# Dilated sliding-window attention and a swish MLP: list-scheduled order on shared PSUM banks, with direct and crossbar loads and half-row scores

## The chip, the cores and the metric

The kernel runs on one core of a Trainium2 chip. The metric is the time of one execution on the device in microseconds; the kernel before takes 364.86 us, the median of three runs (363.77 to 367.04). All times below that are not that median come from one profiled execution of 364.4 us. The engines are called PE (TensorE, matrix products), ACT (ScalarE), DVE (VectorE), POOL (GpSimd) and SP (the engine that issues most DMAs).

## The reference

Two steps. First attention for 8 batches, 8 heads, 576 positions, 64 features per head, in which each head sees 32 keys only:

```python
rel = pos[:, None] - pos[None, :]
mask_plain = (rel >= 0) & (rel < 32)                     # heads 0 to 3
mask_dil = (rel >= 0) & (rel < 128) & (rel % 4 == 0)     # heads 4 to 7
scores = np.where(mask, q @ k.T / 8.0, -1e9)
attn = softmax(scores)                                   # over the keys
attn_out = attn @ v                                      # (8, 8, 576, 64)
```

Then its result, laid out as x with 4608 tokens of 512 features, goes through an MLP with 2048 hidden units and a gate with one beta for each unit:

```python
h = x @ w_in                                             # 512 -> 2048
g = h * (1 / (1 + exp(-beta * h)))
out = g @ w_out                                          # 2048 -> 512
```

Inputs and output are fp32. Both kernels multiply in bf16 and use 0.5 (1 + tanh(beta h / 2)) for the sigmoid.

## The kernel before

The MLP works on nine tiles of 512 tokens ("stages", t = 0 to 8). For each tile there are 16 blocks of hidden units; a block is four 512-column matmuls, a tanh on ACT, and a gate on DVE:

```python
def slot_h(t, fb):
    hps = bank() if t == 0 and fb % 3 else psum_h.tile([P, NTOK], FP32, name="h_ps")[:]
    for kt in range(NKT):                                # 4
        nc.tensor.matmul(hps, lhsT=w_in_bf[:, kt, fb * P:(fb + 1) * P],
                         rhs=xT[:, kt, t * NTOK:(t + 1) * NTOK], ...)
    nc.scalar.activation(out=tnh[:], in_=hps, func=ACT.Tanh, scale=beta_half[:, fb:fb + 1])
    nc.vector.scalar_tensor_tensor(out=g[:], in0=tnh[:], scalar=1.0, in1=hps, op0=ALU.add, op1=ALU.mult)
```

Then four output blocks of 128 tokens, 16 matmuls of 512 columns each, with a copy out of PSUM and a store (`slot_o`, in four parts). Part of the output blocks is put off into the next stage: `at_once = [4, 2] + [1] * (NTT - 3) + [4]` says how many blocks a stage does itself.

Attention of batch 0 runs ahead of all this. Attention of batch t + 1 is cut into steps that are laid between the MLP's slots of stage t, in a fixed list of names. Index x = 0, 1 stands for the two pairs of plain heads, x = 2, 3 for the two pairs of dilated heads, for which positions are split by their remainder mod 4, so that the dilated window becomes a plain one.

```python
STEPS = ("K0 Q0 K1 Q1 S00 S01 S02 S10 V00 S11 V01 S12 X00 V10 S20 X01 V11 S21 X10 S22 V20 X11 S23 "
         "V21 S30 V22 X20 S31 V23 S32 V30 X21 S33 V31 V32 X30 V33 X31").split()
```

- K, Q (plain heads): fp32 loads into a staging buffer, a cast (POOL), eight PE transposes of 72 columns, a copy out of PSUM. Q is written twice, into a tile whose other half is zero (`qz`), so that one matmul with 128 rows gives the scores of both heads of a pair side by side.
- K, Q (dilated heads): a casting DMA into a DRAM scratch (`cast_dil`), then a DMA that transposes on its way into SBUF (`load_dil`), then a copy of Q into the zero-padded `qzd` (`spread_dil`).
- S: scores, exp, mask.
- V: values, with a column of ones that gives the softmax's sum; reciprocal; normalisation.
- X: PE transposes back into the feature-by-token layout of xT, and a copy.

```python
def step_s(b, x, j):
    ...
    for a in range(2):          # n = 96 (plain) or 72 (dilated), both heads side by side: 2 n columns
        nc.tensor.matmul(sc[:, a, 0:2 * n], lhsT=lhsT, rhs=rhs, start=True, stop=True)
    nc.scalar.activation(out=w, in_=sc[:, :, 0:2 * n], func=ACT.Exp, scale=SCALE)
    eng = nc.gpsimd if b > 1 else nc.vector
    eng.tensor_tensor(out=w, in0=w, in1=mask, op=ALU.mult)

def step_v(b, x, j):
    n, m = (QT, 3) if x < 2 else (HT, 2)
    for a in range(m):
        for h2 in range(2):
            ...
            nc.tensor.matmul(pv[:, a, h2, :], lhsT=pt[x][:, c:c + P], rhs=rhs, start=True, stop=True)
    nc.vector.reciprocal(out=rcp[0:n, 0:m], in_=pv[0:n, :, :, D])
    nc.vector.tensor_tensor(out=xs[...], in0=pv[0:n, :, :, 0:D], in1=rcp[...], op=ALU.mult)
```

PSUM has eight banks, given away by use: two for h, one for output blocks, five for attention.

```python
psum_h = psum("psum_h", 2)
psum_o = psum("psum_o", 1)
psum_at = psum("psum_at", 5)
```

The start, in the order of the program: plain K and Q of batch 0 (fp32, SP), casts of dilated K and Q of batches 0 and 1 into DRAM, their transposing loads, V, masks, and only then `load_w_in`; attention 0; `load_w_out`.

Of the kernel before, what the change touches and what calls it, by code (L numbers as in the profile page):

```python
# [13 lines left out]

STEPS = (
    "K0 Q0 K1 Q1 S00 S01 S02 S10 V00 S11 V01 S12 X00 V10 S20 X01 V11 S21 X10 S22 V20 X11 S23 "
    "V21 S30 V22 X20 S31 V23 S32 V30 X21 S33 V31 V32 X30 V33 X31"
).split()  # L20


STEPS_FIRST = (
    "K0 Q0 K1 S00 Q1 S01 S02 S10 S11 S12 S20 S21 S22 S23 S30 V00 S31 V01 S32 X00 "
    "V10 S33 X01 V11 V20 X10 V21 X11 V22 X20 V23 V30 X21 V31 V32 X30 V33 X31"
).split()
# [3 lines left out]
def kernel(  # L30
# [10 lines left out]
    nc = tc.nc  # L41
# [5 lines left out]
    SCALE = 1.0 / 8.0  # L47
    WIN = 32
    C = 4
    CT = S // C  # L50
    HT = CT // 2
    R = 8
    RT = S // R
# [6 lines left out]
    WG = 512  # L60
    FROM = 4
    DV = 96
    GATES = (1,)

    pool = lambda name, bufs: ctx.enter_context(tc.tile_pool(name=name, bufs=bufs))
    psum = lambda name, bufs: ctx.enter_context(
        tc.tile_pool(name=name, bufs=bufs, space=bass.MemoryType.PSUM))
    ctx.enter_context(tc.manual_schedule())

    const_pool = pool("const", 1)  # L70
    stage_pool = pool("stage", 1)
    qkb_pool = pool("qkb", 1)
    dil_pool = pool("dil", 2)
    dram_pool = ctx.enter_context(tc.tile_pool(name="dram", bufs=1, space=bass.MemoryType.DRAM))
    xs_pool = pool("xs", 2)
    rcp_pool = pool("rcp", 4)
    g_pool = pool("g", 2 * NFB)
    tnh_pool = pool("tnh", 3)
    osb_pool = pool("osb", 2)
    psum_h = psum("psum_h", 2)  # L80
    psum_o = psum("psum_o", 1)
    psum_at = psum("psum_at", 5)

    def bank(dt=FP32):
        b = psum_at.tile([P, 512], FP32, name="at")
        return b[:] if dt == FP32 else b[:].bitcast(BF16)

    const = lambda shape, dt, name: const_pool.tile(shape, dt, name=name)
    w_in_bf = const([P, NKT, DFF], BF16, "w_in_bf")
# [5 lines left out]
    mask_p = {n: const([P, 2, 2, C, QT // C], BF16, f"mask_{n}") for n in ("FP", "PP")}  # L95
    mask_d = [const([P, 2, 2, HT], BF16, f"mask_d{hf}") for hf in range(2)]
    kT = [const([P, WIN + S], BF16, f"kT{x}") for x in range(2)]

    qz = [const([P, 2, S], BF16, f"qz{x}") for x in range(2)]
    qzd = [const([P, 2, 2, 4, CT], BF16, f"qzd{i}") for i in range(2)]  # L100
    pt_w = [NI * 2 * QT, NI * 2 * QT, 8 * 2 * HT, 8 * 2 * HT]
    pt = [const([P, pt_w[x] + 64], BF16, f"pt{x}") for x in range(4)]
    vp = [const([P, NI, 4, DV], BF16, f"vp{i}") for i in range(2)]
    vd = [const([P, 2, 4, C, DV], BF16, f"vd{i}") for i in range(2)]
    vp_st = const([P, NI, 4, D], FP32, "vp_st")
    vd_st = const([P, 2, 4, C, D], FP32, "vd_st")
    xT = const([P, NKT, B * S], BF16, "xT")
    warm = const([P, 1], FP32, "warm")
    gate_t = const([1, 16], BF16, "gate_t")


    def zeros():
        nc.vector.memset(warm[:], 0.0)
        nc.scalar.activation(out=warm[:], in_=warm[:], func=ACT.Exp)
        for x in range(4):
            nc.vector.memset(pt[x][:, pt_w[x]:], 0.0)
            if x < 2:
                nc.vector.memset(kT[x][:, 0:WIN], 0.0)
                nc.vector.memset(qz[x][64:128, 0], 0.0)
                nc.vector.memset(qz[x][0:64, 1], 0.0)  # L120
        for i in range(2):
            nc.vector.memset(qzd[i][64:128, 0], 0.0)
            nc.vector.memset(qzd[i][0:64, 1], 0.0)
            nc.vector.memset(vp[i][:, :, :, D:D + 1], 1.0)
            nc.vector.memset(vd[i][:, :, :, :, D:D + 1], 1.0)
            nc.vector.memset(vd[i][96:128, 0, :, :, 0:D], 0.0)
        nc.vector.memset(vp[0][0:WIN, 0, 0, 0:D], 0.0)
        nc.vector.memset(vd_st[96:128, 0], 0.0)

    def build_masks():  # L130

        pp = mask_p["PP"]
        flat = pp[:].rearrange("p a b T u -> p (a b) T u")
        nc.gpsimd.memset(flat, 1.0)
        nc.gpsimd.affine_select(
            out=flat, in_=flat, pattern=[[0, 4], [-1, C], [-C, QT // C]], base=-1,
            channel_multiplier=1, compare_op=ALU.is_ge, fill=0.0)
        nc.gpsimd.affine_select(
            out=flat, in_=flat, pattern=[[0, 4], [1, C], [C, QT // C]], base=WIN,
            channel_multiplier=-1, compare_op=ALU.is_ge, fill=0.0)  # L140
        nc.vector.tensor_copy(out=mask_p["FP"][:], in_=pp[:])
        nc.vector.memset(mask_p["FP"][0:WIN, 0], 0.0)

        for hf, lo in ((0, 0), (1, HT - 16)):
            flat = mask_d[hf][:].rearrange("p a b n -> p (a b) n")
            nc.gpsimd.memset(flat, 1.0)
            nc.gpsimd.affine_select(
                out=flat, in_=flat, pattern=[[0, 4], [1, HT]], base=lo,
                channel_multiplier=-1, compare_op=ALU.is_ge, fill=0.0)
            nc.gpsimd.affine_select(  # L150
                out=flat, in_=flat, pattern=[[0, 4], [-1, HT]], base=WIN - 1 - lo,
                channel_multiplier=1, compare_op=ALU.is_ge, fill=0.0)

    def build_beta():
        tpb = bank()
        nc.tensor.transpose(tpb[:, 0:NFB], beta_row[:, :], ident_f[:, :])
        nc.vector.tensor_single_scalar(
            out=beta_half[:], in_=tpb[:, 0:NFB], scalar=0.5, op=ALU.mult)

    def load_w_in(g):  # L160
        nc.gpsimd.dma_start(
            out=w_in_bf[:, :, g * WG:(g + 1) * WG],
            in_=moe_w_in[:, g * WG:(g + 1) * WG].rearrange("(c p) d -> p c d", p=P))

    def load_w_out(g):
        nc.gpsimd.dma_start(
            out=w_out_bf[:, g * 4:(g + 1) * 4, :],
            in_=moe_w_out[g * 4 * P:(g + 1) * 4 * P, :].rearrange("(c p) d -> p c d", p=P))


    stage, qkb = {}, {}

    def load_qk(b, kind):
        src = {"q": q, "k": k}[kind][b, 0:4].rearrange("h (t T) d -> t h (T d)", T=R)
        dst = stage[b, kind] = stage_pool.tile([RT, 4, R * D], FP32, name=f"{kind}_st")

        for lo, hi in ((0, 64), (64, RT)) if b < 2 else ((0, RT),):
            nc.sync.dma_start(out=dst[lo:hi], in_=src[lo:hi])


    scratch, dil = {}, {}

    def cast_dil(b, kind):
        dst = scratch[b, kind] = dram_pool.tile([CT, 4 * C * D], BF16, name=f"{kind}d{b}")
        nc.gpsimd.dma_start(
            out=dst[:], in_={"q": q, "k": k}[kind][b, 4:8].rearrange(
                "h s d -> (h s d)").rearrange("(a e) -> a e", e=4 * C * D))


    def load_dil(b, kind):  # L190
        dst = dil[b, kind] = dil_pool.tile([P, 2, 4, CT], BF16, name=f"{kind}dT")
        nc.sync.dma_start_transpose(  # L192
            out=dst[:].rearrange("p r h t -> p r (h t)"),
            in_=scratch[b, kind][:].rearrange("a e -> (a e)").rearrange("(a e) -> a e", e=C * D))

    def spread_dil(b, eng):
        for hf in range(2):
            rows = slice(64 * hf, 64 * hf + 64)
            eng.tensor_copy(out=qzd[b % 2][rows, hf], in_=dil[b, "q"][rows])  # L199


    def cast_qk(b, kind, hp, eng):
        if hp == 0:
            qkb[b, kind] = qkb_pool.tile([RT, 2, R, 2, D], BF16, name=f"{kind}b0")
        for h2 in range(2):
            (eng.copy if eng is nc.scalar else eng.tensor_copy)(  # L206
                out=qkb[b, kind][:, hp, :, h2, :],
                in_=stage[b, kind][:, 2 * hp + h2].rearrange("p (T d) -> p T d", T=R))


    def plain_v(b, h4):
        return bass.AP(tensor=v.tensor, offset=v[b, h4].offset - WIN * D,
                       ap=[[D, P], [QT * D, NI], [1, D]])


    def load_vp(b):
        for h4 in range(4):
            if b > 1:
                nc.sync.dma_start(out=vp_st[:, :, h4, :], in_=plain_v(b, h4))
            elif b or h4:  # L220
                nc.gpsimd.dma_start(out=vp[b][:, :, h4, 0:D], in_=plain_v(b, h4))
            else:
                src = v[b, h4].rearrange("(i p) d -> p i d", p=QT)
                nc.gpsimd.dma_start(out=vp[b][WIN:P, :, h4, 0:D], in_=src)
                nc.gpsimd.dma_start(
                    out=vp[b][0:WIN, 1:NI, h4, 0:D], in_=src[QT - WIN:QT, 0:NI - 1])
# [16 lines left out]

    def gate(t, fb):
        nc.sync.dma_start(out=gate_t[:], in_=g_t[t, fb][0:1, 0:16])


    def transposes(b, x, kind):
        src = qkb[b, kind]
# [281 lines left out]
```

The softmax here doesn't subtract the row's maximum and nothing guards it: scores larger than these inputs give would overflow.

## Time and profile before

The page gives busy time of each engine, the span in 40 slices, the chain of work that ended last, and groups of instructions. The lines that the prediction reads are shown there. Beside them these rows are used:

| what | count | mean of one | from |
|---|---|---|---|
| MLP matmul, 512 columns | 1152 in the program | 215.7 ns apart in a stream | chain, four in 0.86 us |
| tanh, 128x512 | 144 | 687 ns | groups |
| gate, 128x512 | 144 | 686 ns | groups |
| exp, 128x384 and 128x288 | 48 and 64 | 487 and 411 ns | groups by shape |
| mask on POOL, 128x384 and 128x288 | 36 and 48 | 936 to 998 and 727 ns | groups by shape |
| normalisation, 96x384 and 72x256 | 32 and 64 | 554 and 421 ns, plus 186 and 174 for the reciprocal | groups by shape |
| copy to xT, 128x288 | 64 | 397 ns | groups by shape |
| output block out of PSUM | 36 | 597 ns | groups |
| DMA over the span | 66,751 packets, 45.8 MB | 45,968 under 512 bytes | page |

A matmul's own mean (384 ns) is its latency; the distance between the starts of two is what a stream costs. A busy share is an average over stages that differ much, so the prediction reads the stages one by one.

### The profile page before, as it was taken

The page shows a single profiled execution, that of the slowest core. Times are in us where ns is not written, and L with a number is a line of the kernel's source. Part 1 is how long each engine was busy: PE and PEld are TensorE (multiplying, and loading weights), DVE is VectorE, ACT ScalarE, POOL GpSimd, SP SyncE. Part 2 cuts the span into 40 slices and gives each one's busy share as a digit, 9 for nine tenths or more (in the row PEclk, how much of TensorE's full clock was granted, in tenths as well). Part 3 has the DMA queues.
Part 4 walks back from the last instruction along what each step waited for, and adds up shares of the span by engine and source line. Part 5 has one row for each costly group of instructions (what it writes and reads, how often), then busy time and mean ns, then how long its engine had stood idle before and what let it go on. Part 6 is the DMA issues. An engine that isn't in the chain of part 4 may idle for free.

```text
span 364.4 us, 6201 instructions
## 1 busy us (share of the span) xinstructions
PE 315.1 (86%) x2305; PEld 167.3 (46%) x2305; DVE 205.2 (56%) x440; ACT 197.1 (54%) x380; POOL 149.8 (41%) x204
## 2 busy tenths in 40 slices
PE   0266999885977999989999999899989999999995
PEld 0254455442443555545554545454545444444442
DVE  6477488556641966485648565756576635334400
ACT  1373486354651776567656755575657545435511
POOL 8444740364285438453936493549243200000000
PEclk9999999999996999999999999999999999999998
DMA  7999999898937950983099419831101110111032
GB/s 180 167 242 210 221 205 149 216 219 216 221 76 188 232 81 23 215 222 78 29 220 250 93 33 233 221 82 30 31 29 31 29 31 29 42 47 29 29 75 72
DMA packets 66751, 45.77 MB, mean 126 GB/s; under 512 B 45968, under 2 KB 57248, under 8 KB 66464
## 3 DMA queue, kind: packets, MB, share of 16 engines
q1 hardware_dynamic: 55728, 35.67, 40.8%
q0 software_dynamic: 10992, 9.70, 17.0%
q8 instruction: 18, 0.29, 0.4%
q14 instruction: 13, 0.11, 0.1%
HBM read 40.89 MB, written 14.16 MB: 151 GB/s over the span
## 4 chain that ended last, share of the span: by engine, by line
PE 67%; DMA 10%; DVE 7%; POOL 6%; ACT 4%; issue 3%; SPq 2%; POOLq 0%; ACTq 0%
PE o_ps L376 28%; PE h_ps L345 26%; DMA w_in_bf<-in_moe_w_in_dram 3%; POOL pt L292 3%; DVE qzd L199 3%; PE at L345 3%; DMA qdT<-qd 3%; PE at L306 3%; SPq L192 2%; PE at L288 2%; DMA vd_st<-in_v_dram 2%; DVE g L353 2%; PE h_ps L376 2%; PE at L322 2%; POOL qb L206 2%
## 5 line engine op out<-in xcount | busy, mean ns | idle before, releaser
L353 DVE SCALAR_TENSOR_TENSOR g<-tnh,h_ps 128x512 bf16<-128x512 bf16 x134 | 91.3, 686 | 105.6 <-ACT tnh L350 105.2
L345 PE MATMUL h_ps<-xT,w_in_bf 128*128 128x512 bf16 x536 | 138.4, 384 | 12.0 <-DVE g L353 9.7
L376 PE MATMUL o_ps<-w_out_bf,g 128*128 128x512 bf16 x544 | 139.2, 384 | 2.9 <-ACT osb L381 2.9
L350 ACT ACTIVATE tnh<-h_ps,beta_half 128x512 bf16<-128x512 f32 x134 | 92.1, 687 | 69.6 <-PE h_ps L345 67.2
L345 PEld LDWEIGHTS <-w_in_bf 128*128 128x128 bf16 x576 | 52.7, 99 | 60.4 <-issue 15.7
L376 PEld LDWEIGHTS <-g 128*128 128x128 bf16 x576 | 52.6, 99 | 53.0 <-issue 6.1
L290 ACT ACTIVATE pt<-at 128x288 bf16<-128x288 f32 (+1 forms) x112 | 47.2, 443 | 11.9 <-PE at L288 11.9
L292 POOL TENSOR_TENSOR pt<-pt,mask_d 128x288 bf16<-128x288 bf16 x48 | 34.9, 727 | 41.0 <-ACT pt L290 35.1
L313 DVE TENSOR_TENSOR xs<-at,rcp 72x256 bf16<-72x256 f32 (+1 forms) x96 | 44.6, 465 | 3.3
L306 PEld LDWEIGHTS <-pt 128*128 128x128 bf16 x448 | 26.3, 103 | 20.4 <-POOL pt L292 8.0
L381 ACT ACTIVATE osb<-o_ps 128x512 f32<-128x512 f32 x34 | 20.3, 597 | 27.2 <-PE o_ps L376 27.2
L292 POOL TENSOR_TENSOR pt<-pt,mask_PP 128x384 bf16<-128x384 bf16 x24 | 22.3, 936 | 21.5 <-ACT pt L290 21.4
L332 ACT COPY xT<-at 128x288 bf16<-128x288 bf16 x32 | 12.7, 397 | 26.0 <-PE at L322 26.0
L322 PE MATMUL at<-ident_b,xs 72*128 72x72 bf16 (+1 forms) x224 | 21.6, 209 | 5.7 <-DVE xs L313 5.7
L292 POOL TENSOR_TENSOR pt<-pt,mask_FP 128x384 bf16<-128x384 bf16 x12 | 12.0, 998 | 35.2 <-ACT pt L290 35.2
L309 DVE RECIPROCAL rcp<-at 72x4 f32<-72x4 f32 (+1 forms) x96 | 17.1, 178 | 15.6 <-PE at L306 14.8
L306 PE MATMUL at<-vd,pt 128*128 128x65 bf16 x256 | 19.9, 201 | 6.8 <-POOL pt L292 6.8
L206 POOL CAST kb<-k_st 72x512 bf16<-72x512 f32 x28 | 16.3, 610 | 17.9 <-PE at L306 17.9
L322 PEld LDWEIGHTS <-xs 72*128 72x128 bf16 (+1 forms) x224 | 15.5, 101 | 17.2 <-DVE xs L313 7.7
L239 POOL CAST vd<-vd_st 128x2048 bf16<-128x2048 f32 x8 | 15.3, 1914 | 10.5 <-DMA vd_st<-in_v_dram 10.5
L288 PE MATMUL at<-qzd,kdT 128*128 128x144 bf16 x128 | 18.6, 238 | 0.7 <-DVE qzd L199 0.7
L206 POOL CAST qb<-q_st 72x512 bf16<-72x512 f32 x28 | 16.3, 610 | 4.8 <-DMA q_st<-in_q_dram 4.8
(64 smaller groups left out, 229.0 us busy)
## 6 DMA issues: line engine op xcount, KB each, us to landing
vp_st<-in_v_dram SPq DMA_DIRECT2D x24, 192.0 KB, 6.7
vd_st<-in_v_dram SPq DMA_DIRECT2D x8, 512.0 KB
k_st<-in_k_dram SPq DMA_DIRECT2D x6, 576.0 KB
q_st<-in_q_dram SPq DMA_DIRECT2D x6, 576.0 KB
vd_st<-in_v_dram SPq DMA_DIRECT2D x8, 384.0 KB
kd<-in_k_dram POOLq DMA_DIRECT2D x8, 288.0 KB, 7.7
qd<-in_q_dram POOLq DMA_DIRECT2D x8, 288.0 KB, 8.7
w_in_bf<-in_moe_w_in_dram POOLq DMA_DIRECT2D x4, 512.0 KB, 16.1
```

The costliest lines, as they stand in the source:

```text
L206: (eng.copy if eng is nc.scalar else eng.tensor_copy)(out=qkb[b, kind][:, hp, :, h2, :], in_=stage[b, kind][:, 2 * hp + h2].rearrange("p ( ...
L288: nc.tensor.matmul(sc[:, a, 0:2 * n], lhsT=lhsT, rhs=rhs, start=True, stop=True)
L290: nc.scalar.activation(out=w, in_=sc[:, :, 0:2 * n], func=ACT.Exp, scale=SCALE)
L292: eng.tensor_tensor(out=w, in0=w, in1=mask, op=ALU.mult)
L306: nc.tensor.matmul(pv[:, a, h2, :], lhsT=pt[x][:, c:c + P], rhs=rhs, start=True, stop=True)
L313: nc.vector.tensor_tensor(out=xs_t[b, x, jx][:, a0:a0 + m], in0=pv[0:n, :, :, 0:D], in1=rcp[0:n, 0:m].unsqueeze(3).to_broadcast([n, m, 2, ...
L322: nc.tensor.transpose(xp[:, a * n:(a + 1) * n], xs[:, a].rearrange("p h d -> p (h d)"), ident_b[0:n, 0:n])
L345: nc.tensor.matmul(hps, lhsT=w_in_bf[:, kt, fb * P:(fb + 1) * P], rhs=xT[:, kt, t * NTOK:(t + 1) * NTOK], start=(kt == 0), stop=(kt == NKT ...
L350: nc.scalar.activation(out=tnh[:], in_=hps, func=ACT.Tanh, scale=beta_half[:, fb:fb + 1])
L353: nc.vector.scalar_tensor_tensor(out=g[:], in0=tnh[:], scalar=1.0, in1=hps, op0=ALU.add, op1=ALU.mult)
L376: nc.tensor.matmul(ops[:], lhsT=g_t[t, fb][:, tb * P:(tb + 1) * P], rhs=w_out_bf[:, fb, :], start=(fb == 0), stop=(fb == NFB - 1))
L381: nc.scalar.mul(out=osb[:], in_=ops[:], mul=0.5)
```

## The change

Nearly all of the kernel is written anew around the same computation. The program no longer lists its instructions: it describes operations with their dependencies, durations and the PSUM bank that each needs, and a planner (`Plan`) places them, when the program is built, by priority and earliest start.

```diff
+class Plan:
+    CAPS = {"h": 3, "p": 4, "o": 2, "z": 4, "a": 8, "s": 5, "w": 6}
+    SWITCH = 95
+    NUDGE = {32: -900, 54: 400, 98: -900, 188: -60, ... 1057: -60}
+    LAT = {"PE": 210, "ACT": 45, "DVE": 45, "POOL": 60, "SP": 0}
+    NEAR = {"PE": 40, "ACT": 60, "DVE": 60, "POOL": 60, "SP": 0}
...
-    psum_h = psum("psum_h", 2)
-    psum_o = psum("psum_o", 1)
-    psum_at = psum("psum_at", 5)
+    BANKS = [psum_pool.tile([P, 512], FP32, name=f"bank{i}") for i in range(8)]
+    plan = Plan(range(8))
...
+    act = lambda n: ("ACT", 175 + .834 * n)
+    dve = lambda n: ("DVE", 160 + 1.042 * n)
+    mm = lambda n: n / 2.4 + 2.5
```

All eight banks are shared; CAPS bounds how many each kind of use may hold. Copies and masks may go to either of two engines, whichever ends first by the plan. While PE waits in the first 80 us of the plan, it runs filler matmuls on zeros:

```diff
+    def filler(b):
+        nc.tensor.matmul(BANKS[b][:, 0:256], lhsT=zero[:, 0:P], rhs=zero[:], start=True, stop=True)
+    plan.run(filler, 80000.0)
```

Loads. Batches 0 to 2 (`DIRECT = 3`) load q, k and v with casting DMAs issued by POOL right into bf16 tiles (the first dilated keys by SP in fp32, and a cast), and transpose K and Q on PE: per batch 24 transposes of 96 columns (dilated) and 72 of 64 columns on 64 rows (plain). Batches 3 to 7 cast q and k of all heads into DRAM scratch, and four crossbar DMAs transpose them into SBUF. A small POOL copy that reads an earlier result (`t_pace`) holds back each batch's loads.

```diff
+    def cast(b, z, h0, deps, vt):
+        dst = scratch[b, z, h0] = dram_pool.tile([S * 4 * D], BF16, name=f"s{b}_{z}_{h0}")
...
+        if h0:     # dilated heads: long runs
+            args = [x.rearrange("(a c e) -> c a e", c=16, e=1024) for x in ...]
+        else:      # plain heads: runs of 64
+            args = (dst[:].rearrange("(s h d) -> s h d", h=4, d=D), src.rearrange("h s d -> s h d"))
+    def crossbar(b, z, h0, deps, vt):
...
+        src = scratch[b, z, h0][:].rearrange("(a e) -> a e", e=C * D)
+        return plan.op([("SP", 1300)], lambda e: nc.sync.dma_start_transpose(out=dst, in_=src), ...)
```

Scores. Q is no longer padded with zeros. Each matmul contracts over the 64 rows of one head, and the two heads of a pair stand in the upper and the lower 64 rows, each with its own PSUM bank:

```diff
+    for c in range(2):
+        rows = slice(64 * c, 64 * c + 64)
+        nc.tensor.matmul(bank(gs[2 * n + c])[:, i * P:(i + 1) * P], lhsT=dk[kv][rows, r, h4, 0:P],
+                         rhs=dq[kv][rows, r, h4, 0:P], start=b >= ADDED, stop=b >= ADDED or i == 3)
```

Dilated heads now take 128 of their 144 positions in one tile of queries and keys; the last 16 queries of each remainder, with the 48 keys that they can see, go into an extra tile for two remainders at once (steps T, U, Y: four matmuls of 68 columns, eight of 65, two transposes). Per batch there are 16 half-row matmuls of 128 columns and 24 of 96. From batch 2 on (`PAIRED`) the score steps of two pairs of heads are done together, from batch 3 on (`AT_ONCE`) all the plain scores at once. The masks of batch 0 are added in PSUM by identity matmuls with -65536 outside the window (`ADDED = 1`; only the tail tile keeps a multiplied mask); later batches multiply after the exp, on POOL or DVE.

The way back. Batches 0 and 1 transpose on PE as before. From batch 2 on (`BY_DMA = 2`) normalised rows are stored into DRAM and come back into xT through a crossbar DMA, in two halves of 288 positions:

```diff
+    o = plan.op([("SP", 1300)], lambda e: nc.sync.dma_start_transpose(out=cols, in_=rows[:]), out + dil, ...)
```

Start and end. The planner puts w_in (three loads, the first of 512 columns) behind batch 0's loads, then batch 1's loads, then w_out (two loads). In stage 0 the first four blocks of hidden units (`APART = 4`) start with the dilated half of x. The last output block is computed and stored in three pieces of columns. Tokens keep their natural order in x, so every output block is one store.

## The prediction

> **What bounds the kernel now.** I read the page in the order busy shares, slices, chain, then cut the span at the places where one token tile of the MLP ends (a stage) and asked for busy time and PE waits in each piece.
>
> The page's busy line and its slices:
>
> ```profile
> PE 315.1 (86%) x2305; PEld 167.3 (46%) x2305; DVE 205.2 (56%) x440; ACT 197.1 (54%) x380; POOL 149.8 (41%) x204
> PE   0266999885977999989999999899989999999995
> PEclk9999999999996999999999999999999999999998
> ```
>
> TensorE is the bound from slice 13 on; before that (9.1 us a slice) it stands at 0, 2, 6, 6 and dips again at slices 9, 11 and 12. No other engine is over 56%. The chain says which waits are on the path:
>
> ```profile
> PE 67%; DMA 10%; DVE 7%; POOL 6%; ACT 4%; issue 3%; SPq 2%; POOLq 0%; ACTq 0%
> ```
>
> And in the chain's pieces in order of time, the two long DMA pieces: the first weights, behind the first attention's loads, and a transposing load of the third batch's queries.
>
> ```profile
> 24.99 11.71 DMA w_in_bf<-in_moe_w_in_dram
> ...
> 76.01 9.78 DMA qdT<-qd
> ```
>
> The stage windows (us, then busy us and count of PE, PEld, DVE, ACT, POOL, then granted clock, DMA share, GB/s):
>
> ```profile
> 0.00:36.70 36.70, 13.38 (x145) 10.57 (x145) 23.31 (x72) 14.47 (x32) 20.02 (x38) 1.00 1.12 200
> 36.70:76.00 39.30, 37.30 (x276) 19.51 (x277) 24.90 (x60) 22.00 (x44) 15.44 (x22) 1.00 1.10 200
> 76.00:117.10 41.10, 32.42 (x239) 16.87 (x237) 22.23 (x46) 20.31 (x42) 23.35 (x30) 0.88 0.86 186
> 220.90:256.90 36.00, 33.87 (x274) 18.44 (x272) 22.79 (x46) 22.42 (x44) 19.25 (x25) 1.00 0.51 130
> 292.90:360.20 67.30, 65.89 (x304) 29.55 (x302) 22.00 (x32) 28.55 (x43) 0.00 (x0) 1.00 0.15 44
> ```
>
> The unit of account: four 512-column matmuls follow each other in 0.86 us (the chain), 215.7 ns each. The MLP has 9 x 128 of them, 248.5 us, in either kernel. A full stage is 128 x 215.7 ns = 27.6 us. So the time before splits into 248.5 of MLP and 115.9 of everything else: **head** 36.7 (first MLP matmul); **stage 0** 39.3 - 27.6 = 11.7; **stage 1** holds only 96 of its matmuls (one 32-block is left for stage 2), 41.1 - 20.7 = 20.4; **stage 2** (112 matmuls, ends 149.7) 32.6 - 24.2 = 8.4; **stages 3 to 6** 36.0 + 35.2 + 36.0 + 36.0 - 4 x 27.6 = 32.8; **stages 7 and 8** 67.3 - 304 x 0.2157 = 1.7; **tail** 4.2. Sum 115.9.
>
> In a later stage the overhead is 8.4 us. Its small matmuls can be counted (head pair x = 0..3): K and Q 32 transposes of 72 columns, scores 12 x 192 and 16 x 144, values 56 x 65, back 12 x 96 and 16 x 72. By the formula n/2.4 + 2.5 ns that is 1.04 + 0.99 + 1.00 + 1.66 + 1.03 = 5.7 us. The remaining 2.7 us are waits and ends of batches: the PE waits in that stage name 1.4 us for DVE's gate and 0.7 for POOL's mask.
>
> **What the Trainium skill says.** "TensorE: Matmul & The Clock Gate", section "Wait — 56ns, not 53.3ns?": a warm stream starts a matmul every n/2.4 + 2.5 ns. The trace agrees also for small ones: eight 72-column transposes take 0.26 us (32.5 ns each), six 65-column value matmuls 0.185. The same page, Part 1: an idle array is given half its clock. The trace has two such spells, 3.4 and 6.8 us long, both in stage 1 (its 0.88 above). "TensorEngine Tiling (Array Packing)", section "Key Properties": different tiles run in parallel, and changing the tiling mode drains the array; no tiled matmul is in this trace. "DMA: Bandwidth & Descriptors", Specifications: under 512 B a transfer falls below line rate. The trace's packet records agree: 2048 B packets took 119 ns (17 B/ns), 256 B ones 23 ns (11 B/ns), casting ones that write 128 B 33 ns.
>
> **The change, part by part.**
>
> *Head.* Before, TensorE starts the MLP at 36.7: attention 0 ran from 10.4 (first cast) to 34.9 (last copy to xT), and w_in was issued only at 25.0. After, loads are issued at once, cast on the way into SBUF, and w_in follows batch 0. Costs from the packet records on 16 engines: a 576 KB fp32 load cast in big packets 23.6/16 = 1.48 us; both weights 25.2 us, so 12.6 for w_in and 3.2 for its first quarter; the 2304 small packets of the plain V 2304 x 33 / 16 = 4.8 us. So K and Q 5.9, dilated V about 1.8, plain V 4.8, first w_in 3.2: 15.7, and some 3 us of issue and landing: **19**. ACT and DVE work of attention 0, at their rows' rates (576-column evacuation 0.75, 512-column exp 0.6, 288-column 0.41, normalisation 0.6 to 0.74, xT copy 0.4), sums to about 22 us; over two engines, starting near 7 us, it ends at 18 if nothing waits. The chain K, S, exp, V, norm, X, copy is long, so I add 5: the MLP starts at **23**, a gain of 13.7.
>
> *Attention on TensorE.* Half-row scores use 64 rows, two heads side by side: if pairs overlap, a batch costs 8 x 55.8 + 12 x 42.5 = 0.96 us plus 4 x 31 = 0.12 for the tail of 16 keys, instead of 1.99. Values: 48 x 29.6 = 1.42 instead of 1.66. From batch 3 on (crossbar) K and Q transposes go; from batch 2 on the transposes back go. With the diff's own allowance of 95 ns a mode change, a crossbar batch is 0.96 + 0.12 + 1.42 + 4 x 0.095 = **2.9 us** against 5.7. Batches 1 and 2 still transpose: dilated 24 x 42.5 = 1.02, plain 72 x 29.2 = 2.10. Batch 1: 1.02 + 2.10 + 1.08 + 1.42 + back 1.02 + 12 changes 1.1 = **7.7**; batch 2 without back and with six changes: **6.1**. So the first two stages gain nothing in PE work; what they can gain is waits.
>
> *Waits.* Stages 0 and 1 lost 11.7 - 5.7 = 6 and 20.4 - 5.7 = 14.7 us beyond attention (DMA of batch 2, clock, POOL masks). Eight pooled banks, a planned order and filler matmuls should take most; I leave 3.5 each. Later stages: 2.7 becomes 1.3 (choice: half). Last two stages 1.5, tail 3.2 (the last block is evacuated in parts).
>
> Sum: 23 + (27.6 + 7.7 + 3.5) + (27.6 + 6.1 + 3.5) + 5 x (27.6 + 2.9 + 1.3) + 55.3 + 1.5 + 3.2 = **318 us**.
>
> *Other engines in a 31.8 us stage.* ACT: 16 tanh x 0.69 + exps 5.8 + four outputs 2.4 = 19; DVE: 16 gates x 0.69 + norms 5.8 + some masks = 18 to 22; POOL: masks up to 11 plus issuing 8. None reaches 31.8.
>
> **Rivals.** (1) *DMA becomes the bound.* A crossbar batch costs, by packet records: dilated casts 2 x 1.48, plain casts to DRAM in 64-element runs 2 x 4.8, four crossbars of 1152 packets 4 x 1.65, V 1.8 + 1.6 + 4.8, back writes and crossbars about 5.8, output 3.8: 37 us against a 31.8 us stage. For: that sum, and two queues at a share of 1.1 in the first 76 us. Against: those packets were timed while queues shared the engines (a share over 1 means overlap), so alone they are shorter; and the stage from 220.9 shows 0.51 x 36.0 = 18 us of packets, so DMA has half of each stage free to begin with. If true, about 5 us in each of five stages: 343. (2) *Half-rows don't overlap*, or each change drains more: 1 to 2 us a stage, 326. (3) *The MLP start is held by attention 0* as now, because its chain and not the loads set it: 30 instead of 23, so 325. (4) *The loads were hidden anyway and the planned order mistimes an engine*: a fixed order waits where the plan's durations are wrong; every engine waits for the latest. At 2 us a stage, 335. (5) Better than planned: waits nearly gone, start at 20: 305.
>
> **Range and chances.** To be slower, the change would have to give back 47 us; even rivals 1 and 2 together leave 351. Range 304 to 340, skewed up for the DMA. Faster by over 2% 0.95, within 2% 0.02, slower 0.03.
>
> **What would show it.** First MLP matmul near 23; crossbar stages 31 to 32.5 us apart; PE waits naming DMA in the crossbar stages would speak for rival 1; starts of paired half-row matmuls closer than 10 ns for the overlap; no half-clock spell before the end. The prediction is wrong if stages 2 to 6 come out at 35 us or the start past 30.

## The result, and the profile after

The changed kernel takes **304.44 us** (median of four, 304.37 to 304.52) against 364.31 before in the same comparison: ratio 0.8347, 95% interval 0.8299 to 0.8394. The prediction was 318, range 304 to 340; the time lies just above the range's lower edge.

The page of the kernel after, its busy line, three slice rows and the chain by engine:

```profile
PE 292.8 (97%) x2271; PEld 150.7 (50%) x2307; DVE 187.8 (62%) x424; ACT 170.3 (56%) x306; POOL 88.5 (29%) x126
...
PE   7989999999999999999999999999999999999995
...
PEclk9999999999999999999999999999999999999999
DMA  7999999799769999995699989996160100010122
...
PE 89%; DVE 6%; issue 2%; DMA 1%; ACT 0%; SPq 0%; DVEq 0%
```

TensorE is busy for 90% or more of every slice (7.6 us each) from the fourth to the last but one, and the row of its granted clock shows no drop. DMA's share of the chain went from 10% to 1%, although its engines are full in most slices up to 225 us. The windows after (same columns as before: us; PE, PEld, DVE, ACT, POOL busy and counts; clock; DMA share; GB/s). I cut them where DMA's work changes, because the planner mixes the stages:

```profile
0.00:19.70 19.70, 16.33 (x231) 11.69 (x232) 13.01 (x44) 10.37 (x22) 17.50 (x37) 1.00 1.18 180
19.70:55.00 35.30, 34.51 (x389) 20.02 (x393) 26.44 (x66) 25.09 (x53) 18.30 (x27) 1.00 1.39 201
...
111.30:146.50 35.20, 34.72 (x265) 17.31 (x269) 24.67 (x62) 19.57 (x36) 9.59 (x12) 1.00 1.19 165
...
225.00:299.70 74.70, 74.33 (x371) 35.54 (x376) 27.95 (x42) 34.12 (x53) 0.00 (x0) 1.00 0.12 43
299.70:302.80 3.10, 0.03 (x1) 0.00 (x0) 0.29 (x1) 0.17 (x1) 0.00 (x0) 1.00 0.29 91
```

And all waits of TensorE from the first MLP matmul to the end, the five groups that the trace names (us in total, times, longest):

```profile
PE bank L903 <- issue: 0.8, 5, 0.2
PE bank L728 <- DVE g L882: 0.5, 1, 0.5
PE bank L664 <- ACT kT L239: 0.2, 1, 0.2
PE bank L868 <- issue: 0.2, 1, 0.2
PE bank L664 <- DVE g L882: 0.2, 1, 0.2
```

1.9 us in 280. In the prediction's account the profiled 302.8 us are: head 19.8 (first MLP matmul, the line below); 279.9 from there to 299.7, of which 248.5 is the MLP and **31.4** everything else; tail 3.1.

```profile
19.77 1.09 PE L868 MATMUL bank<-xT,w_in_bf 128*128 128x512 bf16 x3
```

Of the 61.6 us between the two profiled spans, the head gave 36.7 - 19.8 = 16.9, the tail 1.1, and the overhead inside the MLP 75.0 - 31.4 = 43.6 (before: 11.7 + 20.4 + 8.4 + 32.8 + 1.7). How much of these 43.6 is less work on TensorE can be estimated in two ways. By the count of small matmuls, seven batches at 5.7 us are 39.9 before, against 27.1 after (28.3, less two terms named below), so 13 us are work and 31 are waits and lost clock. By the windows, TensorE was idle for 21.7 us from 36.7 to 360.2 before and lost 5 at half clock (0.88 over 41.1 us), and was idle for 3.6 from 19.7 to 299.7 after, so 23 are waits and clock and 20 are work. Waits and clock are the larger part either way.

### The profile page after: what moved, and what is told of

Its sections match the earlier page's. It is cut to its first block, busy times and chain, and to the rows that moved or that the text cites. A ratio compares the mean times of both kernels' runs of the same rounds, so it can differ in the third digit from the quotient of the medians.

```text
span 302.8 us, 5972 instructions
## 1 busy us (share of the span) xinstructions
PE 292.8 (97%) x2271; PEld 150.7 (50%) x2307; DVE 187.8 (62%) x424; ACT 170.3 (56%) x306; POOL 88.5 (29%) x126
## 4 chain that ended last, share of the span: by engine, by line
PE 89%; DVE 6%; issue 2%; DMA 1%; ACT 0%; SPq 0%; DVEq 0%
PE bank L903 40%; PE bank L868 39%; DVE g L882 2%; PE bank L785 2%; DMA beta_row<-in_moe_beta_dram 1%; PE bank L664 1%; PE bank L769 1%; PE bank L692 1%; PE bank L466 1%; PE bank L473 1%; DVE xdm L620 1%; DVE ptt L604 1%; PE bank L654 1%; PE bank L754 1%; PE bank L728 1%
## 5 line engine op out<-in xcount | busy, mean ns | idle before, releaser
L877 ACT ACTIVATE tnh<-bank,beta_half 128x512 bf16<-128x512 f32 x144 | 97.6, 690 | 71.4 <-PE bank L868 68.6
L903 PE MATMUL bank<-w_out_bf,g 128*128 128x512 bf16 (+2 forms) x588 | 136.2, 367 | 1.6 <-issue 0.8
L868 PE MATMUL bank<-xT,w_in_bf 128*128 128x512 bf16 (+1 forms) x568 | 136.1, 376 | 1.0 <-issue 0.2
L882 DVE SCALAR_TENSOR_TENSOR g<-tnh,bank 128x512 bf16<-128x512 bf16 x144 | 97.3, 686 | 62.2 <-ACT tnh L877 61.4
L918 ACT ACTIVATE osb<-bank 128x512 f32<-128x512 f32 (+1 forms) x34 | 20.0, 588 | 31.2 <-PE bank L903 30.4
L600 ACT ACTIVATE pt<-bank 128x384 bf16<-128x384 f32 (+1 forms) x54 | 20.4, 466 | 6.4 <-PE bank L692 4.3
L600 ACT ACTIVATE ptd<-bank 128x512 bf16<-128x512 f32 x32 | 16.6, 602 | 6.6 <-PE bank L664 6.6
L620 DVE TENSOR_TENSOR xsp<-bank,rcp 96x384 bf16<-96x384 f32 x32 | 17.7, 554 | 1.1
L390 POOL DMA_DIRECT2D vp<-in_v_dram x9 | 15.3, 1696 | 0.4 <-DVE dkt L239 0.4
L785 PEld LDWEIGHTS <-pt 128*128 128x128 bf16 x192 | 8.8, 97 | 4.7
## 6 DMA issues: line engine op xcount, KB each, us to landing
s<-in_q_dram POOLq DMA_DIRECT2D x10, 288.0 KB, 9.4
s<-in_k_dram POOLq DMA_DIRECT2D x10, 288.0 KB, 6.5
vp<-in_v_dram POOLq DMA_DIRECT2D x7, 288.0 KB, 17.1
st<-in_q_dram POOLq DMA_DIRECT2D x6, 288.0 KB, 9.8
st<-in_k_dram POOLq DMA_DIRECT2D x5, 288.0 KB, 11.2
```

Of the source, the lines that this page charges most:

```text
L390: {"POOL": nc.gpsimd, "SP": nc.sync}[queue].dma_start(out=out, in_=in_)
L600: nc.scalar.activation(out=w(), in_=sc(), func=ACT.Exp, scale=SCALE)
L620: nc.vector.tensor_tensor(out=dst, in0=p[..., 0:D], in1=r.unsqueeze(len(p.shape) - 1).to_broadcast(list(p.shape[:-1]) + [D]), op=ALU.mult)
L785: nc.tensor.matmul(pv[:, a, h2, :], lhsT=lhs, rhs=vp[kv][:, (2 * x + h2) * NI + 3 * j + a, 0:D + 1], start=True, stop=True)
L868: nc.tensor.matmul(bank(g)[:, a:z], lhsT=w_in_bf[:, kt, fb * P:(fb + 1) * P], rhs=xT[:, kt, xo + a:xo + z], start=(i == 0 and kt == kts[0] ...
L877: nc.scalar.activation(out=th[:, 0:n], in_=bank(g)[:, 0:n], func=ACT.Tanh, scale=beta_half[:, fb:fb + 1])
```

## The experiments

What is in question: did the gain come from less work on TensorE (half rows, crossbar), from waits taken away (banks, order, fillers), or from the loads; and how near was rival 1, the DMA? "Between" below is the time from the first MLP matmul to the last one's end, 279.9 us in the kernel after; it leaves the head out, which varies (last section).

### Half rows

```diff
-rows = slice(64 * c, 64 * c + 64)      # one_half: for the upper head too
+rows = slice(0, 64)
-rows = slice(64 * c, 64 * c + 64)      # full_rows
+rows = slice(0, 128)
```

> The changed kernel in the same planned order, but both heads of a pair take their scores from the lower 64 rows (so the scores of every second head are those of its neighbour: the output is not the reference's). The mode and the number of instructions stay, only the two halves can't run side by side. Theory, the pairs overlap and TensorE is the bound: 8 x 55.8 + 12 x 42.5 = 0.96 us more in each of seven batches, +6.7, so 311. Rival, such work fits into waits that exist anyway: below 306.

> As the run with one half, but every score matmul contracts over all 128 rows (so it adds up the scores of two heads: the output is not the reference's): no overlap and no change of mode. If a change of mode costs the 95 ns that the plan allows, 38 changes in the batches after the head give back 3.6 us: 307.5. If a change costs nothing, 311 as with one half.

One half: 310.05 us (ratio to before 0.8475, 0.8429 to 0.8521), full rows 306.93 (0.8386, 0.8333 to 0.8439). The same step in the kernel after and then in the run with one half, start and length:

```profile
80.22 0.62 PE L664 MATMUL bank<-dq,dk 64*128 64x128 bf16 x16
```

```profile
81.24 1.06 PE L664 MATMUL bank<-dq,dk 64*128 64x128 bf16 x16
```

The same 16 matmuls take 0.44 us less when neighbours use different halves; the prediction's 8 x 55.8 = 0.45. In the trace of the kernel after, the two matmuls of a pair start 3 or 4 ns apart. Between grew by 6.6 us to 286.5, as the 6.7 expected; the timed 5.6 is smaller by the head, which was 0.8 us shorter in the profile. So the pairs overlap fully, and TensorE is the bound: work put on it shows in the time. Full rows take 2.2 us less than one half between, and one wait of 1.1 us for a load stands against them. The 38 changes of mode that were expected are not what the traces hold. Counted there from the first MLP matmul on (one matmul on 64 rows next to one on more), there are 44 changes with one half and 14 with full rows, which are left by transposes on 64 rows. So 30 changes cost 2.2 to 3.3 us, 73 to 110 ns each. The Trainium skill, "TensorEngine Tiling (Array Packing)", Key Properties, says that a change drains the array; this is its price here. Half rows as a whole, overlap minus changes, are worth 306.93 - 304.44 = 2.5 us by the times, but 4.4 by between (284.3 against 279.9), or 3.3 without that wait; the head of the profile with full rows is 1.7 us shorter.

```diff
-    PAIRED = 2
-    AT_ONCE = 3
+    PAIRED = 8
+    AT_ONCE = 8
```

> No nudges, and scores of one pair of heads at a time in all batches, so 12 changes of TensorE's mode a batch instead of 4 to 6 (output unchanged). At 95 ns a change, 46 more changes cost 4.4 us over the run without nudges. If a change of mode is free, within 1 us of it.

309.54 us against 304.42 without nudges: 5.1 by the times, 4.6 by between (286.5 against 281.9). The traces count 76 changes against 42, so 34 more and not 46, as some steps that the edit parts are still planned side by side: 135 to 150 ns each. This edit changes the order of the scores too, so it is the rougher of the two measures; the plan's 95 ns lies in the range of the first and below the second. Grouping the scores is worth about 5 us, at least as much as half rows.

### Banks and order

```diff
-    CAPS = {"h": 3, "p": 4, "o": 2, "z": 4, "a": 8, "s": 5, "w": 6}
+    CAPS = {"h": 2, "p": 2, "o": 1, "z": 3, "a": 8, "s": 5, "w": 6}
```

> The changed kernel with the MLP held to the banks it had before: at most two for h (also in the start), one for output blocks, three for the last stage's blocks; attention may still take any of the eight (output unchanged). Theory, shared banks removed the waits for the gate and the output copy: PE waits named after DVE's gate and ACT's copy come back, 1 us or more a stage, 313 to 320. Rival, the order removed them and not the banks: below 307.

330.19 us (0.9066, 0.8986 to 0.9146): 26 us lost, twice what was expected. TensorE's longest group of waits, and one window of that run:

```profile
PE bank L868 <- DVE g L882: 11.0, 13, 1.6
```

```profile
220.00:260.00 40.00, 32.60 (x169) 14.15 (x172) 15.92 (x35) 15.14 (x26) 0.00 (x0) 0.87 0.21 56
```

A bank of h is filled in 0.86 us, then read by tanh (0.69) and the gate (0.69). With two banks and nothing else to run, TensorE waits for the gate, as it did in the kernel before. The window shows the second half of the price: the waits let the clock fall. A mean of 0.87 over 40 us means a quarter of them at half clock, some 5 us of work lost.

The loss is not spread evenly over the stages, as the expectation had it. The waits for the gate are 3.9 us from 18 to 100, 0.4 from 100 to 220 and 6.7 from 220 to 260. After that there are none, with the same two banks:

```profile
260.00:300.00 40.00, 39.79 (x183) 18.12 (x186) 17.07 (x25) 20.09 (x30) 0.00 (x0) 1.00 0.11 40
```

There the trace shows four matmuls of h and four of an output block in turn. From 243 to 253 it shows blocks of h one behind the other, with 1.5 us of waiting between each two. The kernel before has such turns in its last two stages too (in places two blocks of h together) and ran them on two banks with 1.7 us of overhead. So two banks are enough while other work stands between two blocks of h, and the planner, which plans anew for the smaller limits, had none left. The 26 us are the worth of a third bank for h and a second for outputs (with the wider limits of the first and last stage, which this run took back as well) under this planner's rule. What they are worth in an order made for two banks is not tested.

```diff
-    NEAR = {"PE": 40, "ACT": 60, "DVE": 60, "POOL": 60, "SP": 0}
+    NEAR = {"PE": 1e9, "ACT": 1e9, "DVE": 1e9, "POOL": 1e9, "SP": 0}
```

> The changed kernel, planned by priority alone: each engine takes the ready operation of highest priority even if another could start earlier (output unchanged). It stands for a fixed list without timing. Theory, the earliest-start rule removes the waits: 315 or more, with PE waits of 10 us and more. Rival, any order with eight banks would do: below 308.

341.78 us (0.9369, 0.9291 to 0.9448). Eight banks and priorities alone keep less than half of the gain. Its largest group of waits, and two windows:

```profile
PE bank L868 <- DMA xT<-x: 7.4, 3, 3.5
```

```profile
20.00:60.00 40.00, 31.12 (x313) 18.65 (x317) 16.25 (x42) 19.61 (x42) 22.84 (x34) 0.74 1.20 166
...
180.00:220.00 40.00, 36.19 (x250) 17.21 (x255) 23.09 (x53) 20.11 (x38) 13.19 (x17) 0.91 1.58 170
```

With priority alone TensorE stands behind an operation whose operands are on their way, even if by the plan another could run. Between 20 and 60 us it was idle for 8.9 us, and a mean clock of 0.74 means half its clock for half of that time. Under this planner both the earliest start and the banks are needed; as taking either away loses over 25 us of the 60 gained, their shares need not add up, and I don't split the gain between them. The order of the kernel before with eight shared banks, which would tell more, was not run.

```diff
-    NUDGE = {32: -900, 54: 400, ... 1057: -60}
+    NUDGE = {}
```

> The changed kernel with the planner's table of hand-set nudges empty (output unchanged). It is the base for the runs that change the number of operations. Theory, the planned order is good by itself and the nudges trim it: 304.5 to 307. Rival, the order is what the nudges make it: 310 or more.

304.42 us (0.8356, 0.8294 to 0.8418): the nudges are worth nothing that can be seen in the time. In the profiles between is 2.0 us longer without them (281.9) and the head 1.8 shorter (18.01). The rule makes the order.

### Fillers and the start

```diff
 def filler(b):
-    nc.tensor.matmul(BANKS[b][:, 0:256], lhsT=zero[:, 0:P], rhs=zero[:], start=True, stop=True)
+    pass
```

> The changed kernel in the same planned order, with the filler matmuls on zeros left out (output unchanged). Theory A, fillers matter because they keep TensorE's clock up through attention 0: the trace shows a half-clock spell in the first 10 us, attention 0 ends later, the first MLP matmul comes 1 to 3 us after 19.8 and the time is 305.5 to 307.5. Rival, the head is set by loads and by ACT and DVE and not by TensorE: first MLP matmul within 0.5 us of 19.8, time within 0.5 us of 304.4.

304.62 us (304.16 to 305.5; 0.8329, 0.8282 to 0.8375), first MLP matmul at 20.23. The rival holds: the fillers aren't needed. Without them the array is slow for longer (36 half-row transposes at 12.72 us take 1.17 us instead of 0.78), but ACT and DVE and the loads pace attention 0, and the first MLP matmul moves by 0.46 us.

```diff
     zeros()
+    for g in range(4):
+        load_w_in(g)
     load_vp(0)
...
-    for g in range(4):
-        load_w_in(g)
     load_qk(1, "k")
```

> The kernel before with the four loads of w_in issued before the plain V of batch 0 instead of after attention's casts (output unchanged). Theory, the end of attention 0 (last copy into xT at 34.9) holds the first MLP matmul and not the weights: it moves from 36.7 to 35 at best, the time by 0 to 2 us, or attention 0 is even delayed by the shared DMA engines. Rival, the late weights hold it: first MLP matmul at 30 or earlier, 6 us gained or more.

This is the kernel before with the weights early: 369.29 us against 363.05, slower by 1.4 to 2.8% (1.0208, 1.0139 to 1.0277). First MLP matmul at 43.06 instead of 36.75, and TensorE's longest wait:

```profile
PE at L253 <- DVE kb L206: 20.7, 1, 20.7
```

That wait names the cast of the first keys, on DVE. What held the cast stands in that run's timeline:

```profile
16.38 0.82 POOL L221 DMA_DIRECT2D vp<-in_v_dram  x1 [3.84 <-DMA w_in_bf<-in_moe_w_in_dram]
...
19.06 0.37 DVE L141 COPY mask_FP<-mask_PP 128x384 bf16<-128x384 bf16 x1 [10.39 <-POOL mask_PP L138]
...
19.56 2.23 DVE L206 CAST kb<-k_st 72x512 bf16<-72x512 f32 x4
```

The cast (at 10.38 before) came right after a copy of a mask, for which DVE had been idle 10.39 us. POOL built that mask only after it had issued the loads of plain V, and one of these issues waited 3.84 us for w_in to land. The queries, which are loaded after the keys, were hardly late (their cast began at 14.82, before at 14.46). So the longest wait came through POOL's queue; values and transposing loads were late as well, and the run doesn't show what early weights would do without that queue.

What they could give is bounded by the kernel before: its last copy into xT ends at 34.9, and w_in lands just before 36.75. With attention 0 as it was, weights that are there in time could let the MLP start 1.8 us earlier at most. The head's gain of 16.9 us is therefore mainly attention 0 earlier: in the kernel after, the first keys are cast at 5.45 us (before 10.38), the dilated V is spread at 14.57 (23.02).

### Loads and the way back

```diff
 def both(e):
     dma("POOL", *args)
+    dma("POOL", *more)     # the same cast into a second scratch
```

> The changed kernel in the same planned order, with each cast of q and k into DRAM scratch of batches 3 to 7 issued a second time into a buffer that nobody reads (output unchanged). By packet records of the kernel before that is 2 x 1.5 + 2 x 4.8 = 12.6 us of all DMA engines more per batch. Theory, loads run about one stage ahead and have slack: 304 to 309, later batches slipping first. Rival, DMA is at its limit in these stages: the time grows by most of five times 10 us, 330 or more.

335.08 us (0.9164, 0.9111 to 0.9217): +30.6. My theory of slack is wrong, the rival right. TensorE's waits:

```profile
PE bank L779 <- DVE ptd L614: 11.1, 3, 6.5
PE bank L878 <- DMA xT<-x: 4.8, 1, 4.8
PE bank L764 <- POOL ptt L614: 3.8, 1, 3.8
PE bank L779 <- POOL ptd L614: 1.7, 1, 1.7
```

They name a mask on DVE first, but in that run's chain of waits three pieces of the loads of plain V, 18 to 21 us each, stand in front of it: the last to arrive was a load. So the kernel after sits close to the limit of its loads. From 111.3 us, where batch 5's loads are issued, the DMA slices stay at 9 for about 24 of the 35 us; 12.6 us more fill the stage. It is not quite at that limit: five times 12.6 = 63 us of packets cost 30.6, and some 12 of these are clock (means of 0.91, 0.91, 0.98 and 0.90 in the four windows of 40 us from 80 to 240). The run also keeps POOL, which issues the casts and, behind them, the loads of plain V, busy for 109.8 us instead of 88.5. Whether the 16 engines or POOL's queue is the limit is not separated.

```diff
-    DIRECT = 3      # both without nudges
+    DIRECT = 8      # direct8;  direct2: DIRECT = 2
```

> No nudges, and all eight batches load directly and transpose K and Q on TensorE; nothing goes through the crossbar on the way in (output unchanged). Theory, TensorE is the bound, so what the crossbar took off it comes back: 24 x 42.5 + 72 x 18.3 (the spacing of the half-row transposes in the trace) = 2.3 us in five batches, and more changes of mode: 12 to 14 us over the run without nudges, with a lower DMA share. Rival, the crossbar's DMA is itself close to binding, so direct loads cost less than 5 us.

328.57 us (0.9065, 0.9027 to 0.9102), 24 us over the run without nudges where 12 to 14 were expected. The work is there, and beside it named waits of 8 us, and clock: one of its windows is

```profile
160.00:200.00 40.00, 36.27 (x313) 18.30 (x318) 24.31 (x53) 19.89 (x37) 7.56 (x10) 0.91 0.56 82
```

with DMA at 0.56, so not short of it in total. By the clock of two such windows (0.91 and 0.96) about 5 us of work were lost. What was late were single loads: their issuer, POOL, waited 20.8 us in all for value matmuls to free V's buffer and 10.5 for transposes to free the staging buffers, and in the chain a load of plain V, 8.7 us from 175, stands ahead of this loss. The theory holds in its direction; its size was right only for the work.

> No nudges, and batch 2 too goes through DRAM and the crossbar instead of PE transposes (output unchanged): a try for a faster version. TensorE gives up 24 x 42.5 + 72 x 18.3 ns = 2.3 us: 302 against 304.4 if DMA can carry it. Rival: from 19.7 to 55 us the DMA share is 1.39 already, the way through DRAM comes too late for the stage that needs it, and TensorE waits for it: 306 or more.

310.42 us (0.8549, 0.8502 to 0.8596), slower by 6.0: no faster version. The rival holds, as far as the waits and the window show:

```profile
PE bank L690 <- DMA out_dram<-osb: 2.3, 1, 2.3
PE bank L767 <- DVE ptd L602: 1.9, 2, 1.8
```

```profile
88.00:120.00 32.00, 27.60 (x210) 13.70 (x209) 22.60 (x53) 16.64 (x30) 9.46 (x11) 0.89 1.35 178
```

The first wait names the store of an output block, but L690 is the scores of plain heads, which read only qT and kT, and both come by the crossbar. The weights from kT were loaded at 94.0 and the first matmul with qT ran at 96.36, so the wait was probably for the load of qT. The DMA share was 1.52 and 1.55 in the two windows before this one. Three direct batches and five by crossbar lie between two limits: one batch more through DRAM and loads are late, five fewer and TensorE has more to do and single loads are late too.

```diff
-    BY_DMA = 2      # without nudges; steps Y2 and Y3 added to the list
+    BY_DMA = 8
```

> No nudges, and the way back into xT by PE transposes in all batches instead of DRAM and crossbar (output unchanged). 12 x 42.5 + 8 x 55.8 + 2 x 29 = 1.02 us of TensorE in six batches: 6 us over the run without nudges if TensorE is the bound. If ACT or DVE, which copy 12 more tiles a batch, become it, 10 or more. Rival, hidden: below 2 us.

312.97 us (311.35 to 314.7; 0.8636, 0.8589 to 0.8684), 8.5 over the run without nudges. Its profiled between is 288.0 against 281.9: 6.1 more, just the work on TensorE. ACT went from 157.7 to 170.1 us busy between 19 and 300 and did not become the bound. The 2.4 us beyond lie outside the profiled execution, and I leave them open.

## Why the prediction was right, and where its sizes were off

The direction, the bound and the order of size held: TensorE is the bound before and after, and the range held the time, by 0.4 us at its edge. The sum was 15.2 us above the profiled span. What came is nearest to rival 5, waits nearly gone and a start at 20. Of the signs named, the pairs start 3 or 4 ns apart, no wait in the crossbar stages names a DMA and no half-clock spell shows; stages of 31 to 32.5 us can't be read off, as the planner mixes them. By the sum's terms:

- **Head**, 23 predicted, 19.8 found: 3.2 too much. Attention 0 itself ended where the sum put it (last copy to xT from 22.32 to 22.7). What the sum left out is that the first blocks start with the dilated half of x, so the MLP runs from 19.8, before attention 0 ends. Rival 3 is out.
- **Attention on TensorE**, 28.3 us for seven batches: right to about 1 us, as the 31.4 less 3.6 idle and about 0.4 of batch 0's tail steps leave 27.4. Half-row overlap came as worked out (0.44 against 0.45 us). Changes of mode are fewer than the 38 counted (34 around the scores in the trace) and cost 73 to 150 ns against 95. One miss: the 72 half-row transposes of 64 columns also run in pairs and take 18 ns each (1.32 us in all) and not 29.2, so two direct batches cost 1.6 us less than I put. Two slips are under 0.1 us: batch 2's terms sum to 6.2, and the tail's matmuls have 64 columns and not 68. Rival 2 is out.
- **Waits**, 3.5 + 3.5 + 5 x 1.3 + 1.5 = 15: this is the term that was mis-sized. Taking 28.3 - 1.6 and the 0.4 of tail steps from the 31.4 leaves **4.3**, near the 3.6 of idle time, of which the trace names 1.9. I had halved the waits by choice; banks and order removed nearly all of them, and with them the half-clock spells. The filler matmuls, named beside them, have no part in it (304.62 without). Rival 4 is what the run by priority became, 342, and not what the kernel is.
- **Rival 1, the DMA**: my packet sum of 37 us a stage was, in its own measure, even low (1.19 x 35.2 = 42 us of packets from 111.3 to 146.5). The mistake was to set it against the stage's time: a share over 1 counts the time in which two queues share an engine twice. But the worry was sound. The extra casts and the run with two direct batches show that little is left. The argument "half of each stage is free" spoke of the kernel before and was no answer.
- **Tail**, 3.2 predicted, 3.1 found.

## What to carry to other kernels

When TensorE is the bound, count its work by n/2.4 + 2.5 ns a matmul and then look at its waits before saving matmuls: here waits and clock were 23 to 31 of 43.6 us, and half-row scores 2.5 to 4.4. A result that is read by two engines in turn (0.69 us each, after 0.86 to fill it) needed a third bank here where such blocks follow each other directly; where other work stands between them, two banks ran without a wait. Waits that come close together cost twice, because they can halve the clock for some us after (7.4 us idle in a window of 40 at a mean clock of 0.87), while single waits of 1.4 us in the later stages of the kernel before left it at 1.00. Before you move a load ahead, see what stands behind it in the queue of the engine that issues it; and to learn how much room the loads have, issue some of their traffic twice.

## What the runs showed of the hardware

The head differs between profiles of nearly the same program by up to 1.8 us, and TensorE's warming up explains a part. The Trainium skill, "TensorE: Matmul & The Clock Gate", Part 1, says that the window in which activity is counted runs freely, so the moment of full speed varies. The same four identity matmuls in the kernel after, and then in the run with one half, whose planned order is the same:

```profile
5.93 1.89 PE L654 MATMUL bank<-add_d,ident_b 128*128 128x512 bf16 x4
```

```profile
5.73 1.04 PE L654 MATMUL bank<-add_d,ident_b 128*128 128x512 bf16 x4
```

Slow in one and fast in the other, after the same fillers; the first MLP matmul came at 19.77 and 18.99. The rest of the 1.8 us is not this: with full rows the four matmuls took 1.04 us too, and the MLP began at 18.05. The row of granted clock shows 9 in both first slices, so it doesn't record the state at the start; the length of known matmuls does. The times of the kernel after scatter by 0.15 us only, so how often which state occurs outside the profiles stays open.
